# Attention and experts on one core: twelve of the 26 late half chunks as three products of rounded halves

## The chip, the cores and the metric

The kernel runs on one core of a Trainium2 chip. The metric is the device time in microseconds of one execution. Times below are of that core; a line number such as L241 is a line of the kernel before, and the changed kernel's numbers are higher (L241 is L245 there, L615 is L665, L1425 is L1476).

## The reference

Four batches of attention over channels, then a layer of eight experts with a capacity. Cut to what is computed:

```python
B, N, C = 4, 5056, 256
qn = q / (norm(q, axis=1) + 1e-6);  kn = k / (norm(k, axis=1) + 1e-6)
a = softmax(kn.transpose(0, 2, 1) @ qn / tau)        # 256 x 256 per batch
x = (v @ a).reshape(20224, 256)

logits = x @ w_gate                                   # 8 experts, cap = 2528
for idx in argsort(-logits.flatten()):                # greedy
    tok, e = idx // 8, idx % 8
    if assigned[tok] < 0 and counts[e] < cap:
        assigned[tok] = e; counts[e] += 1
for e in range(8):
    m = assigned == e
    out[m] = relu(x[m] @ w1[e]) @ w2[e]               # 256 -> 1024 -> 256
```

All inputs and outputs are fp32.

## The kernel before

**Attention.** v arrives turned, in chunks of 1024 tokens (b, c), each a tile of 128x2048. Per batch the scores k^T q are summed on PE, softmax gives a, and each chunk's values x = v a are made in pairs of token tiles (`x_tiles`, L241: plain fp32 matmuls of 128x256, two records each in the trace), copied from PSUM by ACT (L245) and stored to x_d in DRAM by half chunks (`store_x`, L251). Batch 0 already uses three products of rounded halves (`x_tiles_0`, L284: vH aH, vH aL, vL aH). The gate's logits come from `logits` (L432: v against the 8 columns a w_gate in g), which PE does for all tokens; DVE transposes them (L435) and copies them to the tile L (L437). The last gate columns are made by `turned_a` and `gates` (L404, L406, L413, L415, L418, L421).

**Late values.** 13 chunks of v, 26 half chunks, are not multiplied until all logits are there. From then on an order written by hand holds (`tc.manual_schedule()`): the class `Order` keeps a clock for PE and one for DVE, each matmul of the main work calls `o.tick`, and `hook` issues from the waiting streams whatever is due by those clocks. So the late values are the filling between the steps of `route` and `compact`.

**route(p)** finds, for expert phase p, the threshold by which 2528 tokens are chosen. DVE opens it (L549 to L606: largest logit per token, its key, a one-hot table oh), then come eight rounds: DVE compares (ge, L650), PE counts (`totals`, ten matmuls L615, then L628 against ones), DVE and ACT make the next thresholds (L635 to L678; the copy of eq is ACT's, L643). `plan` (L1119) starts route(p + 1) as soon as route(p) is done. **compact** then lists the chosen tokens (matmuls L835, L836, L855 on PE; each output is summed by a test on ACT, L873, or DVE, L889; the list's last step is L936 and idx is L953). POOL gathers the listed rows of x (L1198).

**Experts.** Each phase works on chunks of up to 512 tokens. The first (0, 0) has 256; `turn_both` transposes it on PE (L1384), ACT rounds to xH (L1388) and DVE subtracts to xL (L1389). `turn` does the same for some other chunks (L1361); the rest is staged through DRAM (via, xT on SP's queue). `layer1` (L1425: three products of halves, ph from xH and xL) and `layer2` (L1459) follow. The weights' halves are made on ACT (L1176) and DVE (L1179). Before the change the last LATE = 6 pairs of late values are held back until the lists of phase 0 are there (`o.until(("idx", 0))`), and fill the time until the gathers have landed.

The loop that issues the late values, the place that the diff rewrites, is this:

```python
pairs = [(b, c, t) for b, c in TODO for t in range(0, T, 2)]
for at_ in pairs[:-LATE]:
    pair(*at_)
o.until(("ei", 0))
settle()
o.until(("idx", 0))
```

## Time and profile before

| | |
|---|---|
| time, median of 3 runs (lowest to highest) | 1242.12 us (1239.9 to 1242.85) |
| the profiled execution | 1232.93 us, its span 1231.2 us |
| PE busy in the span | 1208.6 us (98%) |
| DVE, ACT, POOL busy | 872.8 (71%), 560.3 (46%), 395.0 (32%) |
| first late value | 220.53 us |
| first round of route(0) on PE | 234.88 us |
| first matmul of layer 1, chunk (0, 0) | 322.55 us |

The times inside the execution are from the span's start. The profiled execution was 9.2 us shorter than the median of the runs, so a sum made from its rows is first set against its own time. In the rows, an engine's idle time before an instruction and what ended it stand in brackets; a row with xN is N instructions of one line in a row.

### The profile page before, as it was taken

To read this page: it belongs to the slowest core of one execution; us is meant where nothing else is said; L and a number is where in the kernel's file an instruction comes from. 1 tells how busy PE (TensorE), PEld (TensorE's weight loads), DVE (VectorE), ACT (ScalarE), POOL (GpSimd) and SP (SyncE) were. 2 spreads that over 40 slices of the span, in tenths; PEclk is the share of its full clock that TensorE was granted. 3 is DMA by queue.
4 is the path that set the end of the run, shared out by engine and by line. 5 is a ranking of instruction groups with operands and counts; after the bars stand their busy time and mean duration, and the time that the engine had idled before them with its cause. 6 is when DMAs were issued, how large, how long until landed. Compare 5 with 4: busy or idle time off the path is not lost.

```text
span 1231.2 us, 23522 instructions
## 1 busy us (share of the span) xinstructions
PE 1208.6 (98%) x8797; PEld 1101.6 (89%) x8797; DVE 872.8 (71%) x2414; ACT 560.3 (46%) x1301; POOL 395.0 (32%) x663
## 2 busy tenths in 40 slices
PE   7999999999999999999999999999999999999998
PEld 6889977888889999898989999989989998998998
DVE  6788695879689888979878987888766335435431
ACT  6567652235344453435343554463366435334331
POOL 1000000000353452254424443443353345344322
PEclk9999999999999999999999999999999999999999
DMA  8998985235323331332412252342243234322311
GB/s 304 357 398 310 395 322 188 103 123 204 124 95 118 113 101 66 133 95 85 148 63 87 85 184 74 116 137 90 71 148 132 78 112 166 111 81 95 115 65 34
DMA packets 67699, 179.37 MB, mean 146 GB/s; under 512 B 11008, under 2 KB 33920, under 8 KB 62976
## 3 DMA queue, kind: packets, MB, share of 16 engines
q1 hardware_dynamic: 40528, 98.58, 22.3%
q0 software_dynamic: 17664, 58.22, 14.5%
q10 hardware_dynamic: 9392, 21.06, 4.4%
q8 instruction: 69, 1.13, 0.4%
q14 instruction: 46, 0.38, 0.1%
HBM read 118.06 MB, written 59.77 MB: 144 GB/s over the span
## 4 chain that ended last, share of the span: by engine, by line
PE 81%; DVE 9%; issue 5%; POOL 2%; ACT 1%; DMA 1%; POOLq 0%; SPq 0%; DVEq 0%; ACTq 0%
PE py L1459 29%; PE ph L1425 28%; PE s L320 9%; PE px L241 8%; PE px L284 2%; PE pc L615 2%; POOL out_dram L1470 1%; PE px L432 1%; DVE hL L1434 1%; DMA xg<-x_d,src 1%; DVE acc_q L330 1%; DVE acc_k L330 1%; DVE xL L1293 1%; DMA ua<-in_q_dram 1%; DVE m L549 1%
## 5 line engine op out<-in xcount | busy, mean ns | idle before, releaser
L1459 PE MATMUL py<-ua,hH 128*128 128x256 f32 (+1 forms) x2560 | 439.2, 277 | 0.0
L1425 PE MATMUL ph<-xH,ua 128*128 128x512 f32 (+3 forms) x1312 | 395.7, 377 | 4.1 <-DVE hL L1434 3.8
L1459 PEld LDWEIGHTS py<-ua,hH 128*128 128x128 f32 (+1 forms) x2560 | 389.8, 191 | 1.4
L1459 PE MATMUL py<-ua,hL 128*128 128x256 f32 (+1 forms) x1280 | 353.1, 276 | 0.0
L1434 DVE SCALAR_TENSOR_TENSOR hL<-ph,hH 128x512 fp32r<-128x512 f32 (+3 forms) x328 | 217.7, 666 | 138.2 <-ACT hH L1429 137.5
L1429 ACT ACTIVATE hH<-ph 128x512 fp32r<-128x512 f32 (+3 forms) x328 | 190.9, 583 | 199.5 <-PE ph L1425 193.9
L1425 PEld LDWEIGHTS ph<-xH,ua 128*128 128x128 f32 x1312 | 246.3, 190 | 35.4 <-DVE hL L1434 6.9
L1470 POOL DMA_INDIRECT out_dram<-y,idx x160 | 161.8, 1011 | 305.3 <-ACT y L1468 256.2
L1425 PE MATMUL ph<-xL,ua 128*128 128x512 f32 (+3 forms) x656 | 246.9, 376 | 1.8 <-DVE xL L1293 1.8
L1459 PEld LDWEIGHTS py<-ua,hL 128*128 128x128 f32 (+1 forms) x1280 | 244.2, 191 | 0.0
L1198 POOL DMA_INDIRECT xg<-x_d,src x160 | 160.4, 1003 | 99.6 <-issue 46.9
L1468 ACT ACTIVATE y<-py 128x256 f32<-128x256 f32 (+1 forms) x160 | 61.5, 385 | 272.4 <-PE py L1459 220.8
L320 PE MATMUL s<-ua 128*128 128x256 f32 (+1 forms) x640 | 144.8, 386 | 6.9 <-DMA ua<-in_q_dram 6.9
L320 PEld LDWEIGHTS s<-ua 128*128 128x128 f32 (+1 forms) x640 | 121.8, 193 | 26.4 <-issue 10.6
L1425 PEld LDWEIGHTS ph<-xL,ua 128*128 128x128 f32 x656 | 124.9, 190 | 17.6 <-DVE xL L1293 3.9
L329 ACT ACTIVATE sq<-ua 128x1024 f32<-128x1024 f32 (+1 forms) x80 | 76.3, 970 | 49.8 <-DVE acc_k L330 16.4
L1293 DVE TENSOR_TENSOR xL<-xT,xH 128x256 fp32r<-128x256 f32 (+1 forms) x140 | 51.8, 417 | 36.6 <-ACT xH L1289 35.9
L1209 POOL COPY spacer<-hH 1x1 f32<-1x1 f32 x129 | 27.4, 212 | 154.5 <-ACT hH L1429 135.9
L245 ACT ACTIVATE xs<-px 128x512 f32<-128x512 f32 x60 | 35.8, 597 | 66.8 <-PE px L241 66.6
L350 POOL TENSOR_SCALAR ny<-ny 128x4 f32<-128x4 f32 x4 | 2.0, 505 | 182.3 <-ACT ny L349 182.3
L1179 DVE TENSOR_TENSOR ua<-ub,ua 128x512 fp32r<-128x512 f32 x64 | 47.2, 744 | 11.3 <-ACT ua L1176 9.9
L1289 ACT ACTIVATE xH<-xT 128x256 fp32r<-128x256 f32 (+1 forms) x140 | 54.2, 454 | 1.3 <-DMA xT<-via 1.3
(317 smaller groups left out, 1399.8 us busy)
## 6 DMA issues: line engine op xcount, KB each, us to landing
x_d<-xs ACTq DMA_DIRECT2D x40, 512.0 KB, 3.0
ua<-in_k_dram SPq DMA_DIRECT2D x35, 512.0 KB, 6.9
ua<-in_q_dram SPq DMA_DIRECT2D x35, 512.0 KB, 7.6
via<-xs SPq DMA_DIRECT2D x34, 512.0 KB, 2.8
xT<-via SPq DMA_DIRECT2D x136, 128.0 KB, 2.8
vr<-in_vt_dram SPq DMA_DIRECT2D x14, 1024.0 KB, 9.2
ua<-in_vt_dram SPq DMA_DIRECT2D x4, 1024.0 KB, 4.8
xg<-x_d,src POOLq DMA_INDIRECT x160
```

The costliest lines, as they stand in the source:

```text
L241: mm = PE.matmul(px[:, i * C:i * C + width], lhsT=vs[b, c][:, kb, t + i, :], rhs=a_f[b][:, kb, 0:width], start=(kb == 0), stop=(kb == 1))
L320: newest[0] = PE.matmul(sb[:, ib * C:(ib + 1) * C], lhsT=kt[:np_, t, ib * 128:(ib + 1) * 128], rhs=qt[:np_, t, :], start=(first and t == 0 ...
L329: S.activation(sq[:n, t0:t1], t_[:n, t0:t1], AF.Square)
L1198: P.indirect_dma_start(out=xg[:n, i, :], out_offset=None, in_=rows, in_offset=bass.IndirectOffsetOnAxis(ap=routed[p]["src", col][:n, col:c ...
L1289: S.activation(hi[:, a], rows[:, a], AF.Copy)
L1293: V.tensor_tensor(lo[:, a], rows[:, a], hi[:, a].bitcast(F32), op=OP.subtract)
L1425: PE.matmul(ph[:, 0:nt], lhsT=l[:, w], rhs=in_turn(x_, kb, nt).rearrange("p a m -> p m a"), start=(i == 0), stop=(i == 5))
L1429: S.activation(hH[:, fb, 0:nt], ph[:, 0:nt], AF.Relu)
L1434: V.scalar_tensor_tensor(hL[:, fb, 0:nt], ph[:, 0:nt], 0.0, hH[:, fb, 0:nt].bitcast(F32), op0=OP.max, op1=OP.subtract)
L1459: PE.matmul(py[:n, 0:C], lhsT=l[:, fb, tk], rhs=w, start=(j == 0), stop=(j == 23))
L1468: S.activation(y[:n], py[:n, 0:C], AF.Copy)
L1470: sd = P.indirect_dma_start(out=out, out_offset=bass.IndirectOffsetOnAxis(ap=routed[p]["idx", col][:n, col:col + 1], axis=0), in_=y[:n], i ...
```

## The change

Six of the thirteen late chunks (CLOVEN, batches 1 and 2) are cut in twelve half chunks, and each is multiplied as three products of rounded halves (`x_tiles_cut`, L558 of the kernel after); the other seven (PLAIN) stay plain. TURNS gives the order: C is one such half chunk, F two plain pairs. The rounded high half of v is an ACT copy (L546). The low half is made without DVE: ACT writes the negated rounded copy (L543) and a transfer issued by POOL adds v to it from DRAM (L544, accumulating). The halves of a for batches 1 and 2 are made in the same way (L526, L527, L530, L531). PLACES says which buffers take the halves, and BEHIND how far in TURNS a half chunk's copies have to wait. Three half chunks are cut, and the halves of both a made, ahead of the first late value. route(1) may now start only after the lists of phase 0 (`idx`, 0).

```diff
@@ -67,7 +67,11 @@
 GATES_AT = (3, 3)
 FIRST_LAT = 3000
 HOMES = {(1, 0): "ub", (1, 1): "ub", (2, 4): "ua", (3, 0): "ua", (3, 1): "ua", (3, 2): "ua", (3, 3): "late", (3, 4): "late"}
-TODO = ((2, 4), (3, 0), (3, 1), (3, 2), (1, 2), (1, 3), (1, 4), (2, 0), (2, 1), (2, 2), (2, 3), (3, 3), (3, 4))
+PLAIN = ((3, 0), (3, 1), (3, 2), (2, 2), (2, 3), (3, 3), (3, 4))
+CLOVEN = ((1, 2), (1, 3), (1, 4), (2, 4), (2, 0), (2, 1))
+TURNS = "CCFFCFCFCFCFCFCFCCFCCFF"
+PLACES = ("ub", "ub", "vr", "ub", "vr", "ub", "vr", "ub", "ua", "ua", "vr", "ua")
+BEHIND = {3: "C", 5: "CC", 7: "CCCC", 9: "FF", 11: "FFFF"}
 CUT = (4, 4, 4, 4, 4)
 FIRST_CUT = (2, 4, 4, 4, 4, 2)
 PE_TO_DVE = 340
@@ -511,6 +515,52 @@
             job(*j)
 
     rt = ctx.enter_context(tc.tile_pool(name="rt", bufs=1))
+    hctx = ExitStack()
+    hp = hctx.enter_context(tc.tile_pool(name="hp", bufs=1))
+    a_two = {}
+
+    def halve_a(b):
+        a = a_f[b][:, :, 0:C]
+        h, lo = a_two[b] = [hp.tile([128, 2, 2, 128], F32R, name=f"{n}{b}") for n in ("aH", "aL")]
+        less = x_rows()[:, 0:2].bitcast(F32R)
+        S.activation(less, a, AF.Copy, scale=-1.0)
+        P.dma_start(out=less, in_=a, accum_op=OP.add)
+
+        def place():
+            S.activation(h, a.rearrange("p k (m a) -> p a k m", a=2), AF.Copy)
+            S.activation(lo, less.rearrange("p k (m a) -> p a k m", a=2).bitcast(F32), AF.Copy)
+        return place
+
+    cloven = [(b, c, h) for b, c in CLOVEN for h in range(0, T, TH)]
+    v_cut = []
+
+    def cleave():
+        b, c, h = cloven[len(v_cut)]
+        home = PLACES[len(v_cut)]
+        y = (vp.tile([128, 2048], F32, name="vr", bufs=BUFS_V) if home == "vr" else big(home)).bitcast(F32R)
+        y = y.rearrange("p (z k n) -> p z k n", z=2, k=2)
+        raw = vs[b, c][:, :, h:h + TH].rearrange("p k t n -> p k (t n)")
+        S.activation(y[:, 1], raw, AF.Copy, scale=-1.0)
+        P.dma_start(out=y[:, 1], in_=vt[b, c].rearrange("p (k n) -> p k n", k=2)[:, :, h * 128:(h + TH) * 128],
+                    accum_op=OP.add)
+        S.activation(y[:, 0], raw, AF.Copy)
+        v_cut.append(y.rearrange("p z k (t n) -> p z k t n", t=TH))
+
+    def x_tiles_cut(k, t, xs, tick):
+        b = cloven[k][0]
+        px = next_px()
+        aH, aL = a_two[b]
+        for i in range(2):
+            j = 0
+            for kb in range(2):
+                vH, vL = (v_cut[k][:, z, kb, t + i] for z in range(2))
+                for l, r in ((vH, aH), (vH, aL), (vL, aH)):
+                    PE.matmul(px[:, i * C:(i + 1) * C], lhsT=l, rhs=r[:, :, kb].rearrange("p a m -> p m a"),
+                              start=(j == 0), stop=(j == 5))
+                    j += 1
+                    tick(112)
+        S.activation(xs[:, t:t + 2, 0:C], px.rearrange("p (t c) -> p t c", t=2), AF.Copy)
+
     ps_c = ctx.enter_context(tc.tile_pool(name="ps_c", bufs=1, space=PSUM))
     cctx = ExitStack()
     two = [cctx.enter_context(tc.tile_pool(name="two", bufs=2, space=PSUM))]
@@ -1118,7 +1168,8 @@
 
     def plan():
         p = nphase[0]
-        if p < E and done.get(("start", p)) is None and (p == 0 or done.get(("routed", p - 1))):
+        if p < E and done.get(("start", p)) is None and (
+                p == 0 or done.get(("routed", p - 1)) and (p > 1 or done.get(("idx", 0)))):
             done["start", p] = True
 
             def job(p=p):
@@ -1491,20 +1542,49 @@
         want(("ei", 0), first_w)
         rows_of = {}
 
+        def tend():
+            settle()
+            if cut_w[0] and o.pe > cut_w[0][0] and len(cut_w[0]) > 1:
+                split_piece(0, *cut_w[0].pop(1))
+
         def pair(b, c, t):
             if t % TH == 0:
                 rows_of[b, c] = x_rows()
             xs = rows_of[b, c]
             x_tiles(b, c, t, xs, C, o.tick)
-            settle()
-            if cut_w[0] and o.pe > cut_w[0][0] and len(cut_w[0]) > 1:
-                split_piece(0, *cut_w[0].pop(1))
+            tend()
             if t % TH == 2:
                 store_x(b, c, xs, t - 2, t + 2)
 
-        pairs = [(b, c, t) for b, c in TODO for t in range(0, T, 2)]
-        for at_ in pairs[:-LATE]:
-            pair(*at_)
+        pairs = [(b, c, t) for b, c in PLAIN for t in range(0, T, 2)]
+        past = ""
+        place = halve_a(1)
+        cleave()
+        cleave()
+        place()
+        place = halve_a(2)
+        cleave()
+        place()
+        for kind in TURNS:
+            while len(v_cut) < len(cloven) and (len(v_cut) < 3 or len(v_cut) <= len(past) + 2):
+                want_ = BEHIND.get(len(v_cut), "")
+                if any(past.count(x) < want_.count(x) for x in set(want_)):
+                    break
+                cleave()
+            if kind == "F":
+                for t in range(2):
+                    pair(*pairs.pop(0))
+            else:
+                k = past.count("C")
+                b, c, h = cloven[k]
+                xs = x_rows()
+                for t in range(0, TH, 2):
+                    x_tiles_cut(k, t, xs, o.tick)
+                    tend()
+                store_x(b, c, xs, h, h + TH)
+            past += kind
+        assert len(pairs) == LATE
+        hctx.close()
         o.until(("ei", 0))
         settle()
         o.until(("idx", 0))
@@ -1518,7 +1598,7 @@
         for c in range(2):
             load_x(0, c)
         head, queue[:] = list(queue), []
-        for n, at_ in enumerate(pairs[-LATE:]):
+        for n, at_ in enumerate(pairs):
             if n == LATE - 1:
                 queue[:] = head[:HEAD]
                 while queue:
```

By the two builds: 96 plain matmuls become 288 products of halves on PE; ACT has 24 copies of 128x1024 and six of 128x512 more; POOL has 14 adding transfers more (two of 256 KB, twelve of 512 KB); one chunk of tokens, (1, 0), is turned by PE (two more turns) where it was staged through DRAM.

What stands where, first on PE at the end of the logits (g is the gate's columns, turned and ac the last a), before:

```order
L432 MATMUL px<-vr,g_194 32x512 x9
L404 MATMUL pm<-ident,ac 128x128 x4
L432 MATMUL px<-vr,g_194 32x512 x4
L413 MATMUL pm<-wg_t,turned 128x8 x4
L432 MATMUL px<-vr,g_194 32x512 x3
L432 MATMUL px<-ua_1575,g_194 32x512 x2
L432 MATMUL px<-ua_1577,g_196 32x512 x2
```

and after:

```order
L436 MATMUL px<-vr,g_194 32x512 x9
L408 MATMUL pm<-ident,ac 128x128 x4
L436 MATMUL px<-vr,g_194 32x512 x7
L436 MATMUL px<-ua_1575,g_194 32x512
L417 MATMUL pm<-wg_t,turned 128x8 x4
L436 MATMUL px<-ua_1575,g_194 32x512
L436 MATMUL px<-ua_1577,g_196 32x512 x2
```

The gate matmuls stand four logits matmuls later. On DVE the copy that they feed, before:

```order
L435 STREAM_TRANSPOSE turned<-px 128x512
L421 COPY g_196<-ac 128x2x8
L437 COPY L_145<-turned 128x8x16
L435 STREAM_TRANSPOSE turned<-px 128x512
L437 COPY L_145<-turned 128x8x16
```

and after:

```order
L439 STREAM_TRANSPOSE turned<-px 128x512
L441 COPY L_145<-turned 128x8x16
L439 STREAM_TRANSPOSE turned<-px 128x512
L425 COPY g_196<-ac 128x2x8
L441 COPY L_145<-turned 128x8x16
```

The copy to g has a second transposition and its copy ahead of it. On ACT, from the last a to the first evictions of late values, before the change only L406, L415 and L418 stood there; after:

```order
L410 ACTIVATE turned<-pm 128x512
L543 ACTIVATE ub_1817<-vr 128x1024
L546 ACTIVATE ub_1817<-vr 128x1024
L419 ACTIVATE ac<-pm 128x2x8
L422 ACTIVATE a_last<-ac 128x528
L530 ACTIVATE aH_1808<-a_182 128x512
L531 ACTIVATE aL_1809<-xs 128x512
L526 ACTIVATE xs<-a_183 128x512
L543 ACTIVATE vr<-vr 128x1024
L546 ACTIVATE vr<-vr 128x1024
L530 ACTIVATE aH_1823<-a_183 128x512
L531 ACTIVATE aL_1824<-xs 128x512
```

POOL's adding transfers of the same stretch, after (before, its queue had only the memset there):

```order
L527 DMA xs<-a_182 128x2x256
L544 DMA ub_1813<-in_vt_dram 128x2x512
L544 DMA ub_1817<-in_vt_dram 128x2x512
L1067 MEMSET ge 128x2560
L527 DMA xs<-a_183 128x2x256
L544 DMA vr<-in_vt_dram 128x2x512
```

Both halves of a stand on ACT between the last a and the first eviction, and the second a's transfer stands on POOL behind the memset. Last, on DVE ahead of chunk (0, 0)'s xL (L1389, L1440 after), before:

```order
L599 TENSOR_REDUCE eq<-eq 128x8
L601 TENSOR_REDUCE eq<-eq 128x8
L618 TENSOR_TENSOR Dm<-pc,dmask 128x64
L621 TENSOR_REDUCE Dr<-Dm 128x8
L624 TENSOR_TENSOR Ex<-Dr,jsel 120x128
L1389 TENSOR_TENSOR xL<-pt,xH 128x2x128 x2
L635 TENSOR_REDUCE mxs<-pc 128x15
```

and after (m to oh are the opening of route(1); ua is a low half of weights):

```order
L1230 TENSOR_TENSOR ua_2962<-ub_2694,ua_2961 128x512
L616 TENSOR_SCALAR klo<-t_3017 128x160
L619 TENSOR_TENSOR eq<-L_146,m 128x1120
L1230 TENSOR_TENSOR ua_2962<-ub_2694,ua_2961 128x512
L621 TENSOR_TENSOR eq<-eq,code_121 128x1120
L624 TENSOR_REDUCE f<-eq 128x160
L626 TENSOR_TENSOR f<-f,U_147 128x160
L630 TENSOR_TENSOR oh<-f,code_121 128x1280
L1440 TENSOR_TENSOR xL<-pt,xH 128x2x128 x2
L635 TENSOR_SCALAR eq<-ne_151 128x8
```

xL stood in the second round of route(1); it now stands directly behind the opening, ahead of the first round.

## Rows read from the trace of the kernel before

**Rows 1.** the page: busy time by engine; the last chain's shares by engine
```profile
PE 1208.6 (98%) x8797; PEld 1101.6 (89%) x8797; DVE 872.8 (71%) x2414; ACT 560.3 (46%) x1301; POOL 395.0 (32%) x663
...
PE 81%; DVE 9%; issue 5%; POOL 2%; ACT 1%; DMA 1%; POOLq 0%; SPq 0%; DVEq 0%; ACTq 0%
```

**Rows 2.** windows: stretch, us, then busy us of PE, PEld, DVE, ACT, POOL
```profile
220.50:322.50 102.00, 100.33 (x656) 87.49 (x655) 84.74 (x274) 42.05 (x96) 8.46 (x7) 1.00 0.41 155
```

**Rows 3.** timeline of PE (start us, length us, instruction): a round; layer 2
```profile
255.69 0.74 PE L615 MATMUL pc<-oh,ge 128*128 128x64 bf16 x20
256.27 1.54 PE L241 MATMUL px<-a,vr 128*128 128x256 f32 x6
257.46 0.41 PE L628 MATMUL pc<-Ex,ones_q 128*128 128x128 f32 x1
257.71 3.24 PE L241 MATMUL px<-a,vr 128*128 128x256 f32 x14
260.78 0.75 PE L615 MATMUL pc<-oh,ge 128*128 128x64 bf16 x20
...
329.01 0.39 PE L1459 MATMUL py<-ua,hH 128*128 128x256 f32 x2
...
331.69 0.46 PE L1361 MATMUL pt<-identr,xg 128*128 128x128 f32 x4
```

**Rows 4.** timeline of PE, start of the late values and first round
```profile
220.53 7.17 PE L241 MATMUL px<-a,ua 128*128 128x256 f32 x32
...
234.88 0.75 PE L615 MATMUL pc<-oh,ge 128*128 128x64 bf16 x20
```

**Rows 5.** timeline of DVE: the last logits and the start of route(0)
```profile
215.07 0.13 DVE L421 COPY g<-ac 128x16 f32<-128x16 f32 x1
...
218.93 0.72 DVE L435 STREAM_TRANSPOSE turned<-px 128x512 f32<-128x512 f32 x1 [0.69 <-PE px L432]
...
220.65 0.72 DVE L435 STREAM_TRANSPOSE turned<-px 128x512 f32<-128x512 f32 x1 [0.69 <-PE px L432]
...
221.78 2.40 DVE L549 TENSOR_REDUCE m<-L 128x160 f32<-128x1280 f32 x1
...
233.33 1.48 DVE L650 TENSOR_TENSOR ge<-hi,th 128x1200 bf16<-128x1200 int16 x2
```

**Rows 6.** timeline of ACT: one copy of 128 by 512
```profile
212.37 0.60 ACT L406 ACTIVATE turned<-pm 128x512 f32<-128x512 f32 x1 [2.68 <-PE pm L404]
```

**Rows 7.** timeline of POOL at the same place
```profile
221.82 2.23 POOL L1017 MEMSET ge<- 128x2560 bf16 x1 [26.12 <-DVE L L437]
```

**Rows 8.** the page, costliest groups: squares on ACT, 128 by 1024
```profile
L329 ACT ACTIVATE sq<-ua 128x1024 f32<-128x1024 f32 (+1 forms) x80 | 76.3, 970 | 49.8 <-DVE acc_k L330 16.4
```

**Rows 9.** the page, DMA issues: queue, count, KB each, us to landing
```profile
xT<-via SPq DMA_DIRECT2D x136, 128.0 KB, 2.8
vr<-in_vt_dram SPq DMA_DIRECT2D x14, 1024.0 KB, 9.2
```

**Rows 10.** one line's instructions: the gathers on POOL, ns min/median/max
```profile
L1198 POOL DMA_INDIRECT xg<-x_d,src x160: 939/978/1577, 311.5 to 1163.8; - x160
```

**Rows 11.** timeline of PE: the second list's tests, then layer 1's start
```profile
293.58 0.59 PE L855 MATMUL pi<-E__97,G 128*128 128x162 bf16 x6 [0.96 <-DVE G L845]
...
322.55 0.46 PE L1425 MATMUL ph<-xH,ua 128*128 128x256 f32 x1
322.84 0.28 PE L1425 MATMUL ph<-xL,ua 128*128 128x256 f32 x1
```

**Rows 12.** timeline of DVE: route(1) begun, the list's last step, xL
```profile
290.48 2.08 DVE L549 TENSOR_REDUCE m<-L 128x160 f32<-128x1120 f32 x1
...
308.88 0.18 DVE L936 COPY_PREDICATED src<-early,w__2587 128x16 int32<-128x16 int32 x1
...
321.64 0.42 DVE L1389 TENSOR_TENSOR xL<-pt,xH 128x256 fp32r<-128x256 f32 x1 [0.55 <-ACT xH L1388]
```

**Rows 13.** timeline of ACT: the end of the list's last test
```profile
305.02 0.23 ACT L873 ACTIVATION_READ_ACCUMULATOR junk<-pi,rhalf 128x1 f32 x1
```

## The prediction

> **What bounds the kernel now.** First the busy times and the chain of waits [rows 1]: PE is busy 98% of the span and holds 81% of the chain that ended last, so a microsecond counts when it is taken from PE's queue or when PE has to stand still for it. Then the stage that is changed, from 220.5 us (first late value) to 322.5 us (first matmul of layer 1): PE is busy 100.33 of 102.00 us, DVE 84.74, ACT 42.05, POOL 8.46 [rows 2]. PE has 1.67 us of idle time there, so it binds, but DVE is only 17 us behind it. Then the order in that stage: PE's late values are the filling between the rounds of route(0) (L615 to L628), whose answers DVE turns into the next round's thresholds, and between the tests of the two lists; whoever shortens the filling meets DVE's and ACT's chain behind it. Last, the two ends of the stage, one at a time: what must be ready before the first late value [rows 4 to 7], and what before layer 1's second matmul, the first that reads xL [rows 11 to 13].
>
> **PE's own work, by the change's own count.** 96 plain matmuls of 128x256 become 288 products of rounded halves; the other 112 late ones stay. Price of a plain one: from one round's L628 at 257.46 back to 256.27 and on to the next round at 260.78 PE issues ten plain matmuls (20 records, two to a matmul) and one L628, which takes 0.25 (257.46 to 257.71): 4.51 - 0.25 = 4.26, or 0.426 each. Price of a product of halves: 24 of the same shape and type stand between 329.01 and 331.69: 2.68 / 24 = 0.112 [rows 3]. So 96 x 0.426 - 288 x 0.112 = 40.9 - 32.3 = **8.6 us** less on PE. Nothing else leaves the stage's PE but the two rounds of route(1) that stood ahead of layer 1: each is L615 (0.58, from 255.69 to 256.27) and L628 (0.25), 1.7 us together; they go behind its start and are no saving.
>
> **The start, +4.5 us.** Three things stand one behind the other. (a) The gate matmuls L413 (L417 after) now come behind four more logits matmuls. Logits and transpositions go at PE's pace: transpositions begin at 218.93 and 220.65, eight matmuls each, 0.215 a matmul; four make 0.9. The copy of the gate columns to g (215.07) now follows a second transposition and its copy, 1.1 (from 220.65 to the next instruction at 221.78) [rows 5]. Together +2.0, because the rest of the logits need g: they end at 222.5 for 220.53. (b) aH and aL are written where the stage before still has its tiles, so ACT holds them until DVE's last logits copy, 221.7 + 2.0 = 223.7. Two copies at 0.6 [rows 6] and a hand-over of 0.1 follow: the first product starts at **225.0** for 220.53 [rows 4]. The first adding transfers (two low halves of v, one of a) are issued earlier, among the stage before, and are hidden there. (c) The second aL waits for its transfer, which POOL issues behind its memset of 2.23, which moves with the logits from 221.8 to 223.8 [rows 7]: 226.1. The trace has no adding transfer. Its price lies between 2.8 us (128 KB) and 9.2 (1 MB of v) [rows 9], plus a POOL instruction of about 1.0 [rows 10]; 256 KB is nearer to the first, so it lands at 226.1 + 1.0 + 2.8 = 229.9. ACT works in order and stands at that copy with the evictions of the first two half chunks behind it, and PE has two buffers of PSUM: PE is through its first half chunk at 225.0 + 48 x 0.112 = 230.4 and gets its next buffer at 231.1: +0.7 (nothing at best, +7.1 with 9.2). The first round of route(0) stands behind 63 products and 16 plain matmuls: 225.0 + 7.1 + 6.8 + 0.7 = 239.6 for 234.88 [rows 4], **+4.8**; it is PE that is late there, since DVE's table is ready 2 us later than before (233.33 + 1.48 + 2.0).
>
> **ACT's new copies.** 24 of 128x1024 at 0.97 [rows 8] make 23 us in a stage where ACT was busy 42 of 102 [rows 2], so they are hidden as a sum but not in place: six stand in a row ahead of the copy of eq in round 3 and four ahead of that in round 4. I take 0.6 on PE's path (none if ACT has run ahead, 5.8 + 3.9 if it hasn't begun them). SP's queue loses one chunk's staging (the chunk (1,0) is now turned by PE: two more turns) and nothing on the path waits for it; each buffer that a low half goes to is asked for a round or more ahead.
>
> **The end, where the saving stops.** PE's work alone would let layer 1 begin at 322.55 - 8.6 + 4.5 + 0.7 + 0.6 - 1.7 - 0.9 (of the old idle time, which goes with the new order) = **317.1**. But xL on DVE comes later. The second list's tests began at 293.58 [rows 11]; they begin +4.8 + 0.6 later, less 2.1, since DVE's first step of route(1) (290.48, 2.08 us) no longer stands ahead of them [rows 12]: 296.9. From there ACT took until 305.25 [rows 13], 11.7, with evictions and copies of weights between in the same order as now: 308.6. The list's last step ends 1.5 later (eleven DVE instructions 0.13 apart, the last at 308.88 [rows 12]): 310.1, for 309.06 before. Only now may route(1) start, and in DVE's order its whole opening (L599 to L630, ahead of the first round) stands **before** xL. In route(0) that opening went from 221.78 to 233.33, 11.55 [rows 5]; over seven instead of eight experts, by the first step's 2.08 for 2.40, it makes 10.0. Two low halves of weights (under 0.8 each, twice the columns of xL's 0.42 [rows 12]) and the four steps for idx make 1.8. xL starts at 321.9 and its first half is done at 322.3: layer 1's second matmul at **322.4** for 322.84 [rows 11]. Of 5.4 us by which PE would be ahead, 0.4 is left; PE waits the other 5 at layer 1 for DVE.
>
> **Afterwards, +2.4 us.** The two rounds of route(1) that stood ahead of layer 1 now lie within it: +1.7. The two more turns cost PE 0.30 (two, from 331.69 to the next round) to 0.46 each [rows 3]: +0.7. Lists and gathers of later phases come a few us later and had slack. **Sum: -0.4 + 2.4 = +2.0.** On the profiled execution (1232.9, its span 1231.2) that is 1234.9; its own time was 9.2 below the median of the runs, 1242.1, so in the runs' terms 1242.1 + 2.0 = **1244**.
>
> **Rivals.** (1) *xL is not what is last.* If the list ends 4 to 5 us earlier than I have it, PE's work decides: 322.55 - 317.1 = 5.5 saved, less 2.4: 1239. For it: DVE was idle 17 us of the stage, some of which can absorb the delay. Against it: the opening of route(1) stands ahead of xL word for word, whatever comes in. (2) *And the start is hidden too*: the low halves and aH are ready when the logits end. Then another 4.5 stays: 1242.1 - 3.1 - 4.5 = 1234.5. Against it: aH waits for the memory of the stage before. (3) *Slower: the adding transfer of the second a lands late.* Its place is ACT's in-order copy aL2, and it decides from a landing of 4.5 us on (1.7 more than taken, and the sum passes 1245.8). At the 9.2 of the 1 MB load it costs 7.1 for 0.7, all ahead of the first round, so list, route(1) and xL move with it: 1244.1 + 6.4 = 1250; at half of that, 1247. For it: POOL's memset stands ahead, and the load that reads v has that 9.2; against it: the transfers between memories that are nearer in size land in 2.8 [rows 9]. Also for it speaks that a gather on POOL took up to 1577 ns for a median of 978 [rows 10]. The Trainium skill ("SBUF — State Buffer", section "SBUF: two separate sides") has a rule against transfers issued by GpSimd: while DVE runs an operation in a two-port mode, GpSimd can't write the descriptors, and the transfer stands. By that rule aL2 would stand for one of DVE's long steps of route(0); taken as an estimate at the longest, 2.40, this gives 1246.5. No run here shows it yet: the gathers, issued beside a DVE that is busy 71% of the time, lost at most 0.6, so of this rival's chance I give that form 0.05. (4) *The change doesn't do what it says*, the products taking the plain price: 24 of them at 0.112 in the same kernel speak against it [rows 3], and I give it no chance of its own.
>
> **How the numbers follow.** Forecast 0.50 (1244, its own range 1240.5 to 1247.5); rival 1 0.14 (1239, 1236 to 1242); rival 2 0.09 (1234.5); rival 3 0.27 (1250, 1246.5 to 1251). A measurement of this kernel tells 0.3% (3.7 us) from no change: bounds 1238.4 and 1245.8. Faster: rival 2, 0.06 of rival 1 and 0.02 of the forecast, 0.17. Slower: rival 3 and 0.06 of the forecast, 0.33. Same: 0.50. The range leaves out rival 2, the lower quarter of rival 1 and the top of rival 3 (0.09 + 0.03 + 0.05 = 0.17): 1237 to 1250.5.
>
> **What would show it.** In the profile after: the first L558 at about 225, L665 first at about 239.6, with PE idle some 2.5 us ahead of the first product and some 0.7 before its second half chunk; 288 matmuls of L558 at about 0.112 in place of 96 at 0.426; the second list's tests at about 297; and one wait of about 5 us at L1476 (ph from xL) for DVE's L1440. No such wait, with layer 1 at 317, is rival 1; a first product at 221 is rival 2; a wait of 5 us or more at the second half chunk with ACT standing at L531 is rival 3. I am wrong altogether if the rounds of route(0) stretch (ACT's copies ahead of eq cost more than 0.6), or if a later phase stalls on a list or a gather.

## The result and the profile after

The changed kernel took 1252.6 us (median; 1251.95 to 1253.83) beside 1241.5 for the kernel before: ratio 1.0091, 95% interval 1.0073 to 1.0108, 11 us slower. The forecast was 1244, and its range ended at 1250.5.

One thing must be known to read the numbers. The kernel before was timed anew beside each group of runs, and it took 1240 to 1242 us in the first three groups and 1234.5 in the last three; the chip is not shown to decide it, since chip 4 of the record stands beside both levels. The first profile of before, on which the prediction rests, has the shape of the lower level; the times in the table before are of the upper one, and that is most of the 9.2 us between them. A second profile of before (experiment 1) is 7.1 us longer than the first, and 4.7 of these lie in one stretch, layer 1 of phase 1's first two chunks. So like is compared with like below: ratios against the kernel before of the same group, and the trace of after against that second profile.

The page of after, its busy line and the chain's shares, to be held against [rows 1]:

```profile
PE 1206.3 (96%) x8901; PEld 1098.1 (88%) x8901; DVE 874.5 (70%) x2410; ACT 582.8 (47%) x1329; POOL 414.9 (33%) x677
...
PE 74%; DVE 12%; issue 6%; ACT 3%; DMA 2%; POOL 2%; SPq 0%; ACTq 0%; POOLq 0%; DVEq 0%
```

PE is busy 2.3 us less, not 8.6 less, and in a longer span: its idle time is 45 us where it was 23. (Busy time also grows where the clock is low, see below.) DVE's share of the chain rose from 9 to 12%.

PE's timeline of after, at the places of [rows 4] and [rows 11] and at the rounds between:

```profile
224.19 0.38 PE L558 MATMUL px<-aH,ub 128*128 128x256 f32 x1 [1.91 <-ACT aH L530]
...
230.87 7.17 PE L245 MATMUL px<-a_last,ua 128*128 128x256 f32 x32 [0.57 <-ACT xs L562]
...
239.55 0.61 PE L665 MATMUL pc<-oh,ge 128*128 128x64 bf16 x15
...
245.59 0.74 PE L665 MATMUL pc<-oh,ge 128*128 128x64 bf16 x20 [0.63 <-ACT eq L693]
...
256.87 0.74 PE L665 MATMUL pc<-oh,ge 128*128 128x64 bf16 x20 [1.09 <-ACT eq L693]
...
263.30 0.74 PE L665 MATMUL pc<-oh,ge 128*128 128x64 bf16 x20 [0.99 <-ACT eq L693]
...
299.33 0.59 PE L905 MATMUL pi<-E__97,G 128*128 128x162 bf16 x6
...
319.13 0.46 PE L1476 MATMUL ph<-xH,ua 128*128 128x256 f32 x1
323.93 0.58 PE L1476 MATMUL ph<-xL,ua 128*128 128x256 f32 x1 [4.34 <-DVE xL L1440]
...
333.06 0.39 PE L1510 MATMUL py<-ua,hH 128*128 128x256 f32 x2
```

(The view behind the row at 239.55 ends inside the round; a round has 20 records.) The reader sees a late start, three waits for ACT's eq, layer 1 begun early (319.13), and then the wait for xL. DVE's timeline says why xL is late: between the list's last step and xL stands the whole opening of route(1).

```profile
312.01 0.24 DVE L986 COPY_PREDICATED src<-early,w__2853 128x16 int32<-128x16 int32 x1
312.16 2.13 DVE L599 TENSOR_REDUCE m<-L 128x160 f32<-128x1120 f32 x1
...
322.05 1.49 DVE L630 TENSOR_TENSOR oh<-f,code 128x1280 bf16<-128x1280 f32 x1
323.46 0.42 DVE L1440 TENSOR_TENSOR xL<-pt,xH 128x256 fp32r<-128x256 f32 x1
```

Windows around that wait (stretch, its length, busy us of PE, PEld, DVE, ACT, POOL, granted clock, DMA share, GB/s):

```profile
318.00:323.00 5.00, 1.59 (x8) 1.14 (x6) 4.90 (x5) 0.30 (x2) 0.00 (x0) 0.92 0.09 38
323.00:328.00 5.00, 4.07 (x18) 3.91 (x19) 3.83 (x9) 1.64 (x4) 0.00 (x0) 0.50 0.26 105
328.00:332.00 4.00, 3.82 (x43) 3.54 (x43) 1.97 (x6) 1.44 (x4) 1.89 (x2) 0.87 0.22 66
```

After standing 4.3 us PE works at a granted clock of 0.50 (1.2 GHz, the lower of its two levels) for some 5 us; the matmul at 323.93 takes 0.58 where that of [rows 11] took 0.28. Behind layer 1 the waits of PE, summed by what ended them (us in total, times, longest):

```profile
PE pc L678 <- DVE Ex L674: 5.7, 4, 1.8
PE ph L1476 <- DVE hL L1485: 5.7, 8, 1.8
PE ph L1476 <- DVE xL L1440: 4.3, 1, 4.3
PE pt L905 <- DVE ext L1020: 2.1, 2, 1.5
PE pt L1412 <- DMA xg<-x_d,src: 1.6, 1, 1.6
```

In the second profile of before the rounds wait 1.5 us for Ex and the turns 0.3 for gathered rows; those for hL were 5.2; the rest of the list is new or larger. Where the 11 us arise, by the start of the same work in the two traces:

| start of (us) | before, second profile | after | difference |
|---|---|---|---|
| first round of route(0) | 235.4 | 239.6 | +4.1 |
| second list's tests | 294.1 | 299.3 | +5.2 |
| layer 1's second matmul | 323.4 | 323.9 | +0.5 |
| layer 2 of the first chunk | 329.6 | 333.1 | +3.5 |
| layer 1 of phase 0's last chunk | 419.7 | 424.0 | +4.3 |
| layer 1 of phase 1 | 443.3 | 450.5 | +7.2 |
| last start of layer 2 | 1212.1 | 1222.7 | +10.6 |

### The profile page after: what moved, and what is told of

Its sections match the earlier page's. It is cut to its first block, busy times and chain, and to the rows that moved or that the text cites. A ratio compares the mean times of both kernels' runs of the same rounds, so it can differ in the third digit from the quotient of the medians.

```text
span 1251.2 us, 23781 instructions
## 1 busy us (share of the span) xinstructions
PE 1206.3 (96%) x8901; PEld 1098.1 (88%) x8901; DVE 874.5 (70%) x2410; ACT 582.8 (47%) x1329; POOL 414.9 (33%) x677
## 4 chain that ended last, share of the span: by engine, by line
PE 74%; DVE 12%; issue 6%; ACT 3%; DMA 2%; POOL 2%; SPq 0%; ACTq 0%; POOLq 0%; DVEq 0%
PE py L1510 28%; PE ph L1476 25%; PE s L324 8%; PE px L245 3%; PE pc L665 2%; PE px L288 2%; DVE hL L1485 2%; PE px L558 2%; PE px L436 1%; POOL out_dram L1521 1%; DVE acc_q L334 1%; DVE xL L1344 1%; DVE ua L1230 1%; DMA via<-xs 1%; DVE acc_k L334 1%
## 5 line engine op out<-in xcount | busy, mean ns | idle before, releaser
L1249 POOL DMA_INDIRECT xg<-x_d,src x160 | 163.3, 1021 | 91.1 <-issue 48.7
L1260 POOL COPY spacer<-hH 1x1 f32<-1x1 f32 x129 | 30.0, 232 | 155.3 <-ACT hH L1480 141.3
L334 DVE TENSOR_TENSOR acc_k<-acc_k,sq 128x1024 f32<-128x1024 f32 (+2 forms) x40 | 44.3, 1113 | 8.0 <-ACT sq L333 6.7
```

Source lines behind the costliest of these rows:

```text
L334: V.tensor_tensor(acc[:n, t0:t1], acc[:n, t0:t1], sq[:n, t0:t1], op=OP.add)
L1249: P.indirect_dma_start(out=xg[:n, i, :], out_offset=None, in_=rows, in_offset=bass.IndirectOffsetOnAxis(ap=routed[p]["src", col][:n, col:c ...
```

## The experiments

Two theories to begin with. **A**: the loss arises at layer 1's start, by xL behind route(1)'s opening and the low clock after it. **B**: it arises in the later phases, since route(1) starts later (312.2 for 291.0).

**1. The kernel before once more**, for a typical profile. No edit.

> The kernel before, unchanged, for a second profile. Its first profiled execution took 1232.9 us, its timed runs 1240 to 1243, so the first profile is not typical, and 20 us between the two profiles stand against 11 between the medians. Theory A (what the change costs arises up to layer 1's start): up to layer 1, at 322.5 us, this profile agrees with the first within 0.5 us, and its 8 to 9 us more come in the phases of the experts, as waits. Rival (everything runs slower, by clock or memory): the 9 us are spread over all stretches, 2 to 3 of them ahead of layer 1.

1240.3 us, ratio 1.0003 (0.999 to 1.0017). Up to phase 1 its marks are 0.5 to 1.6 us behind the first profile's; then layer 1 of phase 1's first two chunks takes 27.5 us in place of 22.8, with waits of PE, ACT and DVE (1.0, 2.3 and 1.5 us) for nothing that the trace shows; after that the difference stays at 6 to 7. The expected place was right. What makes that stretch longer in some executions stays open.

**2. Chunk (0,0) turned earlier.**

```diff
-            if n == LATE - 1:
+            if n == LATE - 3:
                 queue[:] = head[:HEAD]
```

> The changed kernel with chunk (0,0) turned three late pairs from the end in place of one, so that xL stands on DVE ahead of the last four steps of route(1)'s opening. Theory A (xL behind the opening, and the clock that falls to half in the wait for it, cost 4 us each): layer 1's second matmul at 319.5 to 320.5 for 323.9, granted clock 1.00 behind it, layer 2 from 326 to 327 for 333.1, and 1245 to 1248 in all. Rival B (what counts is that route(1) is late for the later phases): layer 1 starts earlier, but waits of phases 1 to 4 grow by as much, 1251 to 1253.

1254.1 us, ratio 1.0115 (1.0092 to 1.0137): nothing gained, and neither theory's time. The wait for xL is gone, and another stands 5 us further on; first PE, then DVE:

```profile
324.15 0.28 PE L1476 MATMUL ph<-xL,ua 128*128 128x256 f32 x1
...
329.59 0.38 PE L1476 MATMUL ph<-xH,ua 128*128 128x256 f32 x1 [3.38 <-DVE hL L1485]
```

```profile
321.70 0.42 DVE L1440 TENSOR_TENSOR xL<-pt,xH 128x256 fp32r<-128x256 f32 x1 [0.45 <-ACT xH L1439]
...
327.72 1.48 DVE L700 TENSOR_TENSOR ge<-hi,th 128x1200 bf16<-128x1200 int16 x2
329.12 1.08 DVE L1485 SCALAR_TENSOR_TENSOR hL<-ph,hH 128x256 fp32r<-128x256 f32 x3
```

The rest of the opening now stands ahead of hL, and PE is out of PSUM buffers without hL. The granted clock falls here too, to 0.73 on the mean from 331 to 336. By these waits it is the ten microseconds of DVE work, not xL's place in them, that end last. A is wrong as it stood. But the marks of this trace are 2 us late from the start (first product 226.4 for 224.2, tests 301.9 for 299.3; last section), so xL itself came some 4 us earlier than in the change, counted from the tests.

**3. Without the rule on route(1).**

```diff
         if p < E and done.get(("start", p)) is None and (
-                p == 0 or done.get(("routed", p - 1)) and (p > 1 or done.get(("idx", 0)))):
+                p == 0 or done.get(("routed", p - 1))):
```

> The changed kernel without the rule that route(1) waits for the lists of phase 0. Theory A: route(1)'s opening goes back among the list's tests, two rounds stand ahead of xL again, xL is no earlier (322 to 325), so the start of layer 1 gains at most 1 us: 1250 to 1253. Rival B (route(1) late by some 20 us is what the later phases lose): the differences that grow between 424 and 500 us and behind 730 us go, 1242 to 1246, with layer 1's start as late as in the changed kernel.

1244.6 us, ratio 1.0033 (1.0018 to 1.0047): 8 us back by the medians (7 by the ratios), B's number. Layer 1 starts even later (second matmul at 328.1), and at 424 us this kernel is level with the changed one (423.7 and 424.0). All of the gain lies behind: phase 1 starts at 447.4 for 450.5, its layer 2 at 472.3 for 477.6. In DVE's timeline the last step of phase 1's list is where they part. First the second profile of before, then the change without the rule (with its start of route(1)), then the change:

```profile
416.40 0.18 DVE L936 COPY_PREDICATED src<-early,w__3953 128x14 int32<-128x14 int32 x1
```

```profile
298.29 2.14 DVE L599 TENSOR_REDUCE m<-L 128x160 f32<-128x1120 f32 x1
...
421.31 0.18 DVE L986 COPY_PREDICATED src<-early,w__4221 128x14 int32<-128x14 int32 x1
```

```profile
432.68 0.18 DVE L986 COPY_PREDICATED src<-early,w__4264 128x14 int32<-128x14 int32 x1
```

And windows behind it (columns as above), without the rule, then with it:

```profile
424.00:451.00 27.00, 27.00 (x273) 26.31 (x273) 18.77 (x59) 11.30 (x30) 14.50 (x23) 1.00 0.33 102
...
478.00:700.00 222.00, 220.00 (x1834) 203.35 (x1833) 186.60 (x586) 96.02 (x253) 90.73 (x146) 1.00 0.30 97
```

```profile
424.00:451.00 27.00, 24.67 (x247) 24.02 (x245) 19.18 (x62) 9.31 (x28) 14.23 (x21) 1.00 0.20 65
...
478.00:700.00 222.00, 215.48 (x1830) 200.64 (x1830) 184.21 (x587) 93.22 (x251) 86.59 (x141) 1.00 0.29 94
```

PE is idle 2.0 us in these two stretches without the rule and 8.9 with it.

**4. Plain pairs first**, so that PE need not stand for aH; the halves of a are placed behind them.

```diff
-TURNS = "CCFFCFCFCFCFCFCFCCFCCFF"
+TURNS = "FFCCCFCFCFCFCFCFCCFCCFF"
...
```

> The changed kernel with two groups of plain pairs ahead of the first product of halves, and the halves of a made behind them, so that PE need not stand for aH. Theory A: PE starts its late values at 222.3 for 224.2 and does not wait 0.6 us for a buffer, so rounds and lists come 2 to 2.5 us earlier, and so does xL: 1249 to 1251. Rival C (rounds of route(0) go by DVE and ACT, whose copies only move): the first round is earlier, the list's tests are not (299 still), and the time stays 1252 to 1254.

1256.9 us, ratio 1.0136 (1.0114 to 1.0158). The late values start at 222.6, but the first round comes at 239.2, hardly earlier than in the change, and the second waits 2.44 us for eq:

```profile
247.05 0.74 PE L665 MATMUL pc<-oh,ge 128*128 128x64 bf16 x20 [2.44 <-ACT eq L693]
```

Its copy now stands at the end of a long row of work on ACT, from 230.9 on and nearly without a gap: both pairs of aH and aL, evictions, and eight copies of v. Behind the wait the granted clock is low (0.83 on the mean from 245 to 255), and the next round comes 1.6 us later after this one than in the change. The tests begin at 302.4, 3 us later. Rival C is nearer, with a loss that neither expected. The profiled execution took 1252.7 us, the least of the four, so the trace need not hold all of the loss.

**5. The saving by itself**: the kernel before with 20 plain matmuls left out of the late values.

```diff
...
-            for kb in range(2):
+            for kb in range(1 if less and i else 2):
...
```

> The kernel before, with 20 plain matmuls of the late values left out (in 20 pairs of the six chunks one of four; x is then wrong for those tokens, the routing is not): 20 x 0.426 = 8.5 us of PE work taken from the stage at no cost, the saving of the change by itself. Theory F (the late values are filling beside the chain of rounds, lists and route(1), so a shorter filling only moves waits): 1239 to 1241.5, with new idle time of PE ahead of layer 2 or in phase 1. Rival P (PE's saved work reaches the end, and the change's own costs eat it): 1232 to 1234.

1237.3 us, ratio 0.9979 (0.996 to 0.9997): 2.6 of 8.5 us, between the two theories' ranges. Layer 1's second matmul stands at 323.3, where it stood at 323.4; PE waits instead, for a test and for a round:

```profile
304.67 0.24 PE L859 MATMUL pi<-E__97,G 128*128 128x162 bf16 x1 [2.04 <-DVE ext L896]
...
311.50 1.41 PE L619 MATMUL pc<-oh,ge 128*128 128x64 bf16 x20 [3.10 <-DVE ge L654]
...
323.31 0.28 PE L1429 MATMUL ph<-xL,ua 128*128 128x256 f32 x1
```

This is the key run: 8.5 us of PE's work, taken away for nothing, bring layer 1 forward by 0.1. They do not all go into waits. PE's idle time between 220.5 and 323 is 6.8 us for 1.7, and behind the wait of 3.10 its clock falls:

```profile
311.00:317.00 6.00, 5.50 (x31) 4.56 (x31) 3.30 (x9) 0.48 (x1) 0.00 (x0) 0.50 0.04 14
```

The round at 311.5 stands 1.7 us earlier than in the second profile of before (313.2). But it, the five plain matmuls behind it and the round's last matmul take 5.7 us, where the same work took 2.9 at the full clock of that profile: the low clock eats 2.8 us, and from there to layer 1 PE has no gap. So DVE's chain sets the waits, but it is not shown that it would have kept layer 1 at 323 if the clock had held. The 2.6 us of the time do not come from the stage either: layer 1 of phase 1 starts at 443.6 for 443.3, and its first two chunks then take 24.9 us for 27.5, the stretch that differs between executions (experiment 1).

**6. The rule alone, in the kernel before.**

```diff
-        if p < E and done.get(("start", p)) is None and (p == 0 or done.get(("routed", p - 1))):
+        if p < E and done.get(("start", p)) is None and (
+                p == 0 or done.get(("routed", p - 1)) and (p > 1 or done.get(("idx", 0)))):
```

> The kernel before with the new rule alone, route(1) not ahead of the lists of phase 0, and nothing else of the change. Theory H (the rule alone costs the 8 us that the changed kernel got back without it): 1246 to 1250, with layer 1 of phase 1 starting 3 us late or more and xL of chunk (0,0) waited for by 1 us at most. Rival (the rule costs only because the start and the lists were late by then): 1240 to 1243.

1244.3 us, ratio 1.0040 (1.002 to 1.0059), 4.4 us: about half of what theory H said, and more than its rival. The rule has a cost of its own; that the rest of the 8 is paid only beside the late start and list of the change is the likely reading, not a shown one. The marks move by +0.5 at layer 1, +3.5 at phase 1 and +4.4 at the end.

**7. PE kept at work in its wait.**

```diff
+        px = next_px()
+        for j in range(11):
+            PE.matmul(px[:, 0:C], lhsT=vs[3, 4][:, 0, j % T, :], rhs=a_f[3][:, 0, 0:C], start=True, stop=True)
         lctx.close()
```

> The changed kernel with eleven plain matmuls more, whose result nobody reads, ahead of layer 1's first matmul, so that PE works where it waited 4.3 us for xL. Theory (the wait is followed by a stretch at half the granted clock, which costs 3 us): clock 1.00 from 324 to 333, layer 2 from 329.5 to 330.5 for 333.1, and 1249 to 1252 in all. Rival (what follows goes by DVE's hL, whatever the clock): layer 2 at 332 to 334, and 1252 to 1254.

1250.3 us, ratio 1.0091 (1.0059 to 1.0122), which can't be told from the change. In the trace the clock stays at 1.00 through layer 1, and from its second matmul to layer 2 it takes 7.2 us (326.3 to 333.5) for 9.1 (323.9 to 333.1). So the low clock costs 2 us there, not 3. That layer 2 is no earlier for it says nothing: this execution was 2 us behind that of the change at the second list's tests already (301.5 for 299.3).

**8 and 9. What the low halves cost.** Without the rule, first without the negated copies and the adding transfers (8; the third product takes the high half), then with the copies and without the transfers (9). The first line goes in 8 only, the others in both.

```diff
-        S.activation(y[:, 1], raw, AF.Copy, scale=-1.0)
-        P.dma_start(out=y[:, 1], in_=vt[b, c].rearrange("p (k n) -> p k n", k=2)[:, :, h * 128:(h + TH) * 128],
-                    accum_op=OP.add)
...
```

> The changed kernel without the rule on route(1), and without the low halves of v: neither the twelve negated copies nor the twelve adding transfers, and the third product takes the high half again (x is then rounded for these tokens). PE's work is the same. Theory C (ACT's copies ahead of eq and the evictions set the rounds): PE's 2.7 us of waits for eq go, the second list's tests come 2 to 3 us earlier than in the kernel without the rule (301.5), and the time is 1241 to 1243 for 1244.6. Rival (they are hidden beside the rounds): tests within 1 us, 1244 to 1246.

> The changed kernel without the rule on route(1), with ACT's twelve negated copies of v but without the twelve adding transfers, so that the low halves hold the negated high halves (x is wrong for these tokens). The version without either took 1238.1, the one with both 1244.6. Theory C (the copies, which stand in ACT's order ahead of eq and the evictions, are what costs): waits for eq of 2.7 us as before, the second list's tests at about 301, and 1243.5 to 1245.5. Rival T (the transfers cost: a product waits for its low half, or they crowd the stores and gathers): tests at 298.5, and 1237.5 to 1239.5.

8 took 1238.1 us (ratio 0.9984, 0.9974 to 0.9993), 9 1235.3 at the lower level (1.0004, 0.9995 to 1.0014). The second list's tests in 3, 8 and 9:

```profile
301.45 0.59 PE L905 MATMUL pi<-E__97,G 128*128 128x162 bf16 x6 [0.85 <-DVE G L895]
```

```profile
298.49 0.59 PE L902 MATMUL pi<-E__97,G 128*128 128x162 bf16 x6 [0.85 <-DVE G L892]
```

```profile
303.44 0.59 PE L903 MATMUL pi<-E__97,G 128*128 128x162 bf16 x6 [0.84 <-DVE G L893]
```

Without copies, none of the three waits for eq is left, and the tests come 3 us earlier, though the first round does not (240.4 for 240.2). In 9 they are late because that execution lost 1.7 us at the start (last section); the waits for eq are there. To be sure, the three were run beside each other on one chip:

> The changed kernel without the rule on route(1), once more, as the base of the next two on the same chip: the chips differ by 6 us in the kernel before (1240 and 1234.5), most of it in one stretch of phase 1. Both theories: a ratio to the kernel before of 1.002 to 1.005, the second list's tests 7 us later than in the kernel before.

> The same without the adding transfers alone, beside its base. Theory C (ACT's negated copies cost): within 1.5 us of the base. Rival T (the transfers cost): 3 us or more below it, and within 1 us of the kernel without both.

> The same without transfers and negated copies, beside its base. Theory C: 3 to 6 us below the base and 2 to 5 below the kernel with the copies alone; the list's tests 3 us earlier than in both. Rival T: no more than 1 us below the kernel with the copies alone.

1236.6 (1.0022, 1.0012 to 1.0032), 1235.0 (1.0008, 0.9998 to 1.0017) and 1231.4 (0.9972, 0.9962 to 0.9982). The copies cost 3.6 us; the transfers' 1.6 is not clear of noise, since the two intervals overlap. It is mostly C.

**10. The halves cut late**, with the right result: no rule, six plain groups first, one half chunk cut per group.

```diff
-TURNS = "CCFFCFCFCFCFCFCFCCFCCFF"
+TURNS = "FFFFFFCFCCFCCFCCFCCFCCC"
-            while len(v_cut) < len(cloven) and (len(v_cut) < 3 or len(v_cut) <= len(past) + 2):
+            if len(past) > 2 and len(v_cut) < len(cloven) and len(v_cut) < past.count("C") + 4:
...
```

> A version with the right result: no rule on route(1); six groups of plain pairs first, the halves of a made among them, and then one half chunk cut per group, so that nothing of the halves stands ahead of the first late value, and no four or six copies in a row ahead of eq. PE's work is that of the changed kernel. Theory F (PE's saved work is worth nothing at layer 1, since DVE's chain of route(1), list and xL ends last; only the costs can be avoided): first late value at 220.5 to 221.5, second list's tests at 294 to 296, layer 1 from 322 to 324, and 1237 to 1241, not below the kernel with 8.5 us of PE work left out (1237.3). Rival P (with the costs gone the saving shows): layer 1 from 314 to 318, and 1231 to 1235.

1234.2 us beside 1234.6, ratio 1.0005 (0.9996 to 1.0014): no difference. PE has its 8.6 us less to do, none of the costs at the start, and layer 1 starts at 324.6. Its waits there:

```profile
292.74 0.16 PE L885 MATMUL pc<-cb,before 128*128 128x1 bf16 x1 [2.05 <-DVE cb L879]
...
301.57 0.37 PE L905 MATMUL pi<-E__97,G 128*128 128x162 bf16 x3 [1.01 <-ACT ext L926]
307.38 0.24 PE L905 MATMUL pi<-E__97,G 128*128 128x162 bf16 x1 [1.83 <-DVE ext L942]
316.17 0.47 PE L665 MATMUL pc<-oh,ge 128*128 128x64 bf16 x10 [2.89 <-DVE ge L700]
```

With 0.85 and 0.83 more these make 9.5 us: what was saved is now waited. Behind the last of them the clock is low again (0.54 on the mean from 318 to 321, worth 1.5 us). Theory F holds in a kernel with the right result too.

**11. Four low halves of weights on POOL**, added to 10.

```diff
-    SPLIT = [(i, q_, None) for i in range(2) for q_ in range(4)]
+    SPLIT = [(i, q_, P if i else None) for i in range(2) for q_ in range(4)]
```

> The version with the halves cut late (as fast as the kernel before, with 9.5 us of new waits of PE for DVE and ACT between 290 and 320 us), and four of the eight low halves of the first weights subtracted on POOL in place of DVE, where they stand among the list's tests: 4 x 0.69 us off DVE. Theory F (DVE's chain is what ends last, so what comes off DVE comes off the time): PE's waits between 300 and 320 shrink by 2 us or more, layer 1 at 321 to 322.5, and 0.998 to 0.999 of the kernel before. Rival (ACT's tests and the gathers, now behind POOL's work, end as late): layer 1 at 323 to 326, and 0.9995 to 1.002.

1234.4 us, ratio 1.0000 (0.9991 to 1.001). POOL takes 6.38 us for the four, the gathers come behind them (313.0 for 310.6), and xL at 325.5 for 323.8. The rival was right in the time, with layer 1 at 327.0 later still than it said; this run does not show that DVE's work is the bound, since the gathers moved.

**12. One copy of v on ACT**: the products take the negated high half, SP copies it, POOL adds v to the copy. The halves of the second a are made after the sixth half chunk.

```diff
-        S.activation(y[:, 1], raw, AF.Copy, scale=-1.0)
+        S.activation(y[:, 0], raw, AF.Copy, scale=-1.0)
+        nc.sync.dma_start(out=y[:, 1].bitcast(F32), in_=y[:, 0].bitcast(F32))
...
-        S.activation(y[:, 0], raw, AF.Copy)
...
```

> A version with the right result and half of ACT's copies: no rule on route(1); ACT writes only the negated high half of v, SP copies it to the low half's place (twelve plain transfers of 512 KB) and POOL adds v there; the products take the negated half with aH and aL and the low half with a negated aH, and ACT turns the sign as it copies the result out. The halves of the second a are made after the sixth half chunk. Theory C (the second copy of v on ACT is worth 3.6 us, as it was between 1235.0 and 1231.4): 3 to 5 us below the kernel without the rule on the same terms, 0.997 to 0.999 of the kernel before, eq waited for by 1.5 us in all or less, tests at 297.5 to 299.5. Rival (the copy's time comes back as a longer way of the low half: ACT, SP, POOL, three transfers in a row): products wait for their low half, 1.001 to 1.004.

1253.0 us, ratio 1.0151 (1.0138 to 1.0165). The waits for eq are gone, but the second a's low half came late. ACT's copy for it was done at 260.3; POOL, whose queue stood for SP's copies, issued the adding transfer at 271.8, and it took until 283.7 to land:

```profile
284.48 0.58 PE L559 MATMUL px<-aL,vr 128*128 128x256 f32 x1 [14.43 <-ACT aL L531]
```

This one wait is 14.4 of the 16.4 us by which it lies behind the repetition of 3. What the version would take without it was not tried.

**13. The change once more, at the lower level.** No edit.

> The changed kernel once more, beside the version above and the kernel before on one chip. If what the rule on route(1) costs is a matter of order (the waits of the later phases), the ratio is that of the first time, 1.007 to 1.011, whether or not this chip has the 6 us longer stretch in phase 1; if it comes of that stretch, 1.004 to 1.006 on a chip whose kernel before takes 1234.5.

1246.4 us beside 1234.3, ratio 1.0107 (1.0092 to 1.0123). The loss does not hang on the level, so not on the stretch of experiment 1: it is a matter of order.

## Why the prediction failed, step by step

**PE's saving** was sized right (products at 0.112 apart, 8.6 us of work less) and its worth too: the forecast left 0.4 of it at layer 1, experiment 5 left 0.1. The prediction's reason, that DVE's chain ends last there, is half of what the runs show: PE's waits in 2, 5 and 10 are mostly for DVE, but the clock that falls behind them, which the sum did not have, takes 2.8 us in 5 and 1.5 in 10. In part the small number is luck. What the saving is worth with the clock held was not tried.

**The start** came as worked out, to within 0.7 us (the first round +4.1 against the second profile, for +4.8, which is 4.7 by its own numbers). g moved and was waited for, 1.01 us; aH waited for DVE's last logits copy; the first product at 224.19 for 225.0, the second buffer 0.57 late for 0.7, the first round at 239.55 for 239.6. The second aL stood for its transfer by the amount taken, and rival 3 did not come:

```profile
227.06 0.76 ACT L530 ACTIVATE aH<-a 128x512 fp32r<-128x512 f32 x1
229.54 0.79 ACT L531 ACTIVATE aL<-xs 128x512 fp32r<-128x512 f32 x1 [1.72 <-DMA xs<-a]
```

The rule of the Trainium skill that was weighed there ("SBUF — State Buffer", section "SBUF: two separate sides") did not show itself: beside a DVE at work on route(0)'s opening this transfer, issued on POOL at 225.68, had landed by 229.5, as fast as by the row taken without the rule. Whether any of DVE's steps there runs in such a mode is not in the trace, so the rule is not tested by it.

**ACT's copies** were sized wrong: 0.6 us taken, 2.71 measured in three rounds (0.63, 1.09, 0.99). The prediction counted the copies ahead of eq in two rounds; there were three, and the losses went on to the list. Tests at 299.3 for 296.9, xL done at 323.9 for 322.3. Of these 1.6 us 0.5 are the second profile's own lateness; against it layer 1's second matmul stands at +0.5 where the sum had -0.4.

**The wait at layer 1** was foretold (5 us; 4.34 measured) but not its sequel: the granted clock at 0.50 for 5 us, worth 2 us by experiment 7. This step was missing. With one round of route(1), which the sum had, it makes the 3.0 us from there to layer 2 (+0.5 to +3.5).

**"Lists and gathers of later phases come a few us later and had slack"** is the step that failed. From layer 2 of the first chunk to the end the change loses 7.1 us more (+3.5 to +10.6) where the sum had at most 2.4. The two rounds put behind layer 1 and the two more turns were counted; that route(1) starts 21 us later than before, and that phase 1's list ends 16 later (its last step at 432.7 for 416.4), was read as slack, from a trace in which nothing waited for that list. Of the 21 and the 16 the rule alone makes 14 and 11, against experiment 3 (298.3 and 421.3). Experiments 3 and 6 put a price on it: 8 us in the changed kernel (10 by the medians of 13 and of experiment 3's repetition), 4.4 in the kernel before. How the late list turns into this loss is read from the waits and not shown by a run of its own: behind layer 1's start PE waits 5.7 us for Ex in the rounds and 2.1 for ext in the tests, where it waits 1.9 and 1.2 without the rule, and the next lists are late too (phase 2's last step at 542.7 for 534.6). In the repetition, 13, the rounds wait only 2.9 us and the loss is as large, so the place of the waits is not fixed. By the marks, 0.9 at layer 1's second matmul, 3.0 in layer 1 and 7.1 behind it, less the 2.4 that the sum had, make the 8.6 us by which the forecast was short.

**Rival 1 and rival 2** rested on PE's work deciding; experiment 5, in which 8.5 us less of it moved layer 1 by 0.1, speaks against both.

## What to carry to other kernels

Before making filling cheaper, take some of it away and look at what it fills: if the next stage does not move, little can be won there as the order stands, whatever the busy share says; then ask which waits took the gain, and whether the clock fell behind them. A producer that is moved behind a consumer's deadline has to be followed into the next rounds of work, not only to the next wait. And copies that are cheap as a sum are paid where they stand ahead of a small result in an engine's order.

## What the runs showed of the hardware

After the 1.0 us wait for g, among matmuls of 32 columns, the granted clock fell to half in some executions and not in others of the same instructions. The same stretch in experiment 2 and in after:

```profile
218.00:221.00 3.00, 3.00 (x20) 0.87 (x16) 0.01 (x1) 0.00 (x0) 0.00 (x0) 0.50 0.65 117
```

```profile
218.00:221.00 3.00, 3.00 (x33) 0.90 (x26) 1.37 (x3) 0.00 (x0) 0.00 (x0) 1.00 0.43 78
```

Where it fell, the 26 matmuls that follow took 4.89 us for 3.20: 1.7 us. It also fell in the profiled executions of 9 and of its repetition. POOL needed 1.6 us for a subtraction of 128x512 (6.38 for four) that DVE does in 0.69.
